# FNet mixing and a gated convolution FFN on one core: the last multiply-add a step later, the taps first, batch 1's folds moved

## The chip, the core and the metric

The kernel runs on one core of one Trainium2 chip. The metric is the device time of one execution in microseconds, as a median of several runs. TensorE (PE) multiplies matrices into PSUM, VectorE (DVE), ScalarE (ACT) and GpSimd (POOL) work on tiles, and SyncE (SP) issues transfers. Each engine runs its own instructions in the order in which they were written and waits on semaphores for the others.

## The reference

```python
X = np.fft.fft(np.fft.fft(x, axis=1), axis=2).real        # x: (8, 3136, 256)
h = np.maximum(X @ w_in, 0)                               # w_in: (256, 1024)
conv = cw[0]*h[s-1] + cw[1]*h[s] + cw[2]*h[s+1]           # along the sequence, zeros outside
gate = 1 / (1 + np.exp(-conv))
out = (h * gate) @ w_out                                  # w_out: (1024, 256)
```

## The kernel before

All arithmetic is float32. The weights arrive as float64 words and are narrowed to float32 on the core (`narrow`), in parts of four or so VectorE instructions and one of ScalarE.

*Per batch.* A batch of x (3136 x 256) comes in two halves, tiles `xh`: a plain load from SyncE, four gathers of mirrored rows issued by GpSimd (line 132), and for the second half three small loads of row 0 (`zero`, line 126). `fold_ops` gives sixteen VectorE steps, eight for each half, that add and subtract mirrored rows and features (lines 157 to 227); before `turned` ScalarE scales a copy (`scaled`). The result, tile `w`, goes through `units`: matrix products with cosine and sine tables (`tabs`, even and odd), put together on VectorE into `pt` and `qt`, the half-spectrum of the batch. Half of the spectrum is enough, since the other half mirrors it.

*The loop.* The DFT along the features and w_in are multiplied once into `G`. The loop has 256 steps (8 batches x 4 chunks of the sequence x 8 blocks of 128 rows of d_ff). Step s passes through:

| stage | engine | line |
|---|---|---|
| `seed` and `products`: `pa`, `pb` in PSUM | ACT, PE | 760, 93 |
| `copies`, `combine`: `nb`, then the row `h` (with relu) | ACT, DVE | 796, 805 |
| `first_tap`: `g` = tap 0 times h | ACT | 811 |
| `middle`: h added into g by an accumulating DMA (the taps are divided by the middle one) | POOL queue | 815 |
| `last_tap`: the last multiply-add of the convolution | DVE | 820 |
| `sigmoid`, `gate` (GpSimd takes half the row, VectorE the other) | ACT, POOL, DVE | 835, 843, 844 |
| `mm2`: the last product with w_out into `po` | PE | 93 |

The order in which these are written in iteration t is fixed by hand:

```python
    for t in range(n + LAG):                 # LAG = 4
        sigmoid(steps[t - 3]); run("first")
        products(steps[t + 1]); copies(steps[t + 1]); run("act")
        combine(steps[t]); seed(steps[t + 2]); first_tap(steps[t])
        run("dve"); last_tap(steps[t - 2]); gate(steps[t - 3])
        row_of(steps[t + 1]); middle(steps[t]); run("pool"); run("load")
        mm2(steps[t - LAG]); run("pe")
```

`run(...)` puts in what was entered for this iteration with `at(cycle, where, fn)`: the next batch's loads, folds and units, the remaining narrowing of the weights, and the "feature" work (one feature column for all batches). For batch 1 the sixteen folds stand in the free cycles from 4 to 23.

*The prologue.* Batch 0's work comes ahead of the loop. In the order written: `w_cv.load` (the conv taps, on ACT), the first part of w_in (SP), x's two halves, `load_turn` (angles, four loads of single words on ACT, line 287), a ScalarE instruction that negates the angles (line 699), three memsets on GpSimd, the odd tables of one kind (ACT, `load_odd`, lines 274 to 279), the even tables (SP, lines 260 to 265), the odd tables of the other kind (SP), then w_in's rest. After that `w_cv.narrow`, `w_in[0].narrow` and `taps` (a transposing product, the ScalarE copy of line 736 and small VectorE instructions, lines 738 to 744), and then the folds of batch 0. `scaled` writes four tiles from the pool `rp` for batch 0 (`parted`). After the folds `mend_row` and `mirror_tables` (lines 295 and 301) finish the tables on ScalarE, and TensorE runs the units.

Of the kernel before, what the change touches and what calls it, by code (L numbers as in the profile page):

```python
# [37 lines left out]
def kernel(  # L38
# [38 lines left out]
    hp = ctx.enter_context(tc.tile_pool(name="hp", bufs=5))  # L77
    gp = ctx.enter_context(tc.tile_pool(name="gp", bufs=6))
# [63 lines left out]
    def fold_ops(b):  # L142
# [4 lines left out]
        def half(h):  # L147
# [95 lines left out]
    rp = ctx.enter_context(tc.tile_pool(name="rp", bufs=4))  # L243
# [439 lines left out]
    def raw_in(i):  # L683
        def f(sh):
# [6 lines left out]
            for i in range(4)]  # L691
    w_cv.load(nc.scalar)
# [6 lines left out]
    act(turn[0:NP, 2], turn[0:NP, 1], AF.Copy, scale=-1.0)  # L699
# [12 lines left out]
    cw = const.tile([P, 3, NF], F32, name="cw")  # L712
# [20 lines left out]
    def taps():  # L733
        p = spare()
        mm(p[:, 0:3 * NF], cw24[:, 0], ident, True, True)
        nc.scalar.copy(out=cw.rearrange("p k m -> p (k m)"), in_=p[:, 0:3 * NF])
        small = const.tile([P, NF], F32, name="small")
        vt(small, cw[:, 1], cw[:, 1], op=ALU.mult)
        nc.vector.tensor_scalar(out=small, in0=small, scalar1=TINY * TINY, scalar2=2.0 * TINY, op0=ALU.is_lt,
                                op1=ALU.mult)  # L740
        vt(cw[:, 1], cw[:, 1], small, op=ALU.add)
        nc.vector.reciprocal(out=small, in_=cw[:, 1])
        for k in (0, 2):
            vt(cw[:, k], cw[:, k], small, op=ALU.mult)
# [17 lines left out]
    def triple(s):  # L762

        return third(steps.index(s))

    def third(i):

        return False

# [6 lines left out]
    def products(s):  # L776
        b, c, f = s
        ch, n, fs = cut(s)
        pb[s] = psb.tile([P, 512], F32, name="pb", tag="pb")
        mm(pb[s][:, 0:n], G[0:P - 1, 1, fs], PQ[b][1][0:P - 1, ch.k0:ch.k1], True, True)  # L780
        mm(pa[s][:, 0:n], G[:, 0, fs], PQ[b][0][:, ch.k0:ch.k1], False, not triple(s))
        if triple(s):
            mm(pa[s][:, 0:n], G[0:P - 1, 1, fs], PQ[b][1][0:P - 1, ch.k0:ch.k1], False, True)

    def copies(s):

        ch, n, fs = cut(s)
        p = pb.pop(s)
        nb[s] = nbp.tile([P, 2, HN], F32, name="nb", tag="nb")
        if triple(s):  # L790
            act(nb[s][:, 1, ch.cols], p[:, ch.cols], AF.Copy, scale=-2.0)
            row_of(s)
            act(hs[s][:, ch.front], pa[s][:, ch.fcols], AF.Relu)
        else:
            for i, cols in enumerate((ch.fcols, ch.cols)):
                act(nb[s][:, i, cols], p[:, cols], AF.Copy, scale=-1.0 if i else 1.0)  # L796

    def combine(s):

        ch, n, fs = cut(s)  # L800
        a, c = pa.pop(s), nb.pop(s)
        h = hs[s]
        for i, (to, cols) in enumerate(((h[:, ch.front], ch.fcols), (h[:, ch.back][:, ::-1], ch.cols))):
            if i or not triple(s):
                nc.vector._custom_dve(TENSOR_ADD_SAT, out=to, in0=a[:, cols], in1=c[:, i, cols],  # L805
                                      s0=BIG, s1=0.0)
# [15 lines left out]
    def shares(s):  # L822


        ch = chunks[s[1]]
        w = ch.w - 2
        n = ch.rest[0] if ch.last else w
        m = n - n // (4 if third(steps.index(s) + 2) else 2)
        return slice(0, m), slice(m, n), slice(n, w)
# [44 lines left out]
    w_cv.narrow(0, 1)  # L874
    w_in[0].narrow(0, 2)
    taps()
# [119 lines left out]
    for b in range(1, B):  # L996
        ops, singles, pres = fold_ops(b)
        c0, n = ends[b - 1], ends[b] - ends[b - 1]
        if b == 1:

            cs = [c for c in range(4, ends[1] + 1) if c not in taken]
            assert len(cs) == len(ops) and cs[len(ops) // 2] > NF + 4
# [16 lines left out]
    LAG = 4  # L1019
# [7 lines left out]
    for t in range(n + LAG):  # L1027
# [3 lines left out]
        if 0 <= t - 3 < n:  # L1031
            sigmoid(steps[t - 3])
# [94 lines left out]
```

## Time and profile before

| | us |
|---|---|
| three runs | 1188.72, 1190.26, 1190.9 (median 1190.26) |
| the profiled execution | 1192.42, of which its span is 1190.7 |
| busy in the span: PE, DVE, ACT, POOL | 1138.7, 957.9, 945.0, 600.7 |
| granted clock of TensorE, mean | 0.998 |
| read from and written to HBM | 38.40 MB, 25.74 MB |

The page of the profile gives the busy time of each engine and slices of the span; other views give the busy time in chosen stretches, an engine's instructions in order of time with the idle time before each and what ended it, and the waits summed by who waited for whom. An engine that is not the last one waited for may idle without cost.

### The profile page before, as it was taken

Reading aid. Unit: us, or ns where it says so; the run is one execution under the profiler, and the core shown is the slowest. Engines: PE = TensorE matmul, PEld = TensorE weight load, DVE = VectorE, ACT = ScalarE, POOL = GpSimd, SP = SyncE. Lnnn points to the kernel's source line nnn. Section 1 sums busy time; section 2 is a strip of 40 time slices with the busy share of each in tenths; the row PEclk is TensorE's granted clock in tenths of the full one; section 3 lists DMA queues with packets and bytes.
Section 4 is the critical chain, followed back from the end, with each engine's and each line's share of the span. In section 5 each row is a group of like instructions: output and inputs, shape, how many; then the busy total and the mean of one; then the engine's idle time right before and its main releaser. Section 6 shows DMA issues by size and latency. Waiting matters only on the chain.

```text
span 1190.7 us, 16046 instructions
## 1 busy us (share of the span) xinstructions
PE 1138.7 (96%) x4818; PEld 888.1 (75%) x4818; DVE 957.9 (80%) x1448; ACT 945.0 (79%) x1939; POOL 600.7 (50%) x734
## 2 busy tenths in 40 slices
PE   0989899999999999999999999999999999999998
PEld 0656678778777787777778777777777777777776
DVE  3689878988788798988787788998787687787774
ACT  0388777887888788888787888888887888898885
POOL 4335765666364546565646464454444444444443
PEclk9999999999999999999999999999999999999999
DMA  7386696767587667767766576765566556666664
GB/s 200 107 153 134 144 161 159 154 139 156 118 193 148 144 122 169 159 149 154 160 137 138 120 173 141 168 142 122 120 124 123 120 121 137 132 131 129 125 122 103
DMA packets 107586, 168.15 MB, mean 141 GB/s; under 512 B 32657, under 2 KB 62627, under 8 KB 107501
## 3 DMA queue, kind: packets, MB, share of 16 engines
q0 software_dynamic: 41984, 115.83, 51.4%
q1 hardware_dynamic: 64345, 50.89, 15.0%
q8 instruction: 38, 0.62, 0.2%
q10 hardware_dynamic: 1172, 0.43, 0.2%
q14 instruction: 47, 0.39, 0.1%
HBM read 38.40 MB, written 25.74 MB: 54 GB/s over the span
## 4 chain that ended last, share of the span: by engine, by line
PE 79%; ACT 7%; DVE 6%; issue 4%; POOL 2%; DMA 2%; ACTq 0%; POOLq 0%; DVEq 0%; SPq 0%
PE po L93 50%; PE pb L93 12%; PE pa L93 11%; PE pd L93 6%; ACT g L835 2%; DVE g L820 2%; ACT nb L796 2%; POOL xh L132 1%; DMA g<-h 1%; ACT os L868 1%; ACT g L811 1%; DMA out_dram<-os 1%; ACT pa L760 1%; DVE xh L168 0%; DVE g L844 0%
## 5 line engine op out<-in xcount | busy, mean ns | idle before, releaser
L93 PE MATMUL po<-wout,g 128*128 128x256 f32 x3072 | 707.2, 380 | 11.1 <-DVE g L844 10.5
L93 PEld LDWEIGHTS po<-wout,g 128*128 128x128 f32 x3072 | 580.1, 190 | 158.2 <-DVE g L844 28.1
L815 POOL DMA_DIRECT2D g<-h x256 | 228.1, 891 | 470.2 <-ACT g L811 244.7
L835 ACT ACTIVATE g<-g,cw 128x385 f32<-128x385 f32 (+2 forms) x512 | 292.0, 623 | 86.6 <-DVE g L820 85.7
L820 DVE SCALAR_TENSOR_TENSOR g<-h,cw,g 128x770 f32<-128x770 f32 (+1 forms) x256 | 299.1, 1168 | 41.7 <-DMA g<-h 41.6
L843 POOL TENSOR_TENSOR g<-g,h 128x385 f32<-128x385 f32 (+1 forms) x256 | 292.7, 1143 | 54.9 <-ACT g L835 53.8
L796 ACT ACTIVATE nb<-pb 128x386 f32<-128x386 f32 (+3 forms) x512 | 226.6, 497 | 93.9 <-PE pb L93 93.3
L805 DVE CUSTOM_DVE_ANT_0 h<-pa,nb 128x386 f32<-128x386 f32 (+3 forms) x512 | 264.2, 556 | 15.7 <-POOL h L774 11.4
L811 ACT ACTIVATE g<-h,cw 128x770 f32<-128x770 f32 (+1 forms) x256 | 244.0, 953 | 0.0
L93 PE MATMUL pb<-qt,G 127*128 127x387 f32 (+2 forms) x512 | 213.9, 499 | 2.3 <-ACT nb L796 1.3
L93 PE MATMUL pa<-pt,G 128*128 128x387 f32 (+2 forms) x512 | 211.9, 494 | 1.7 <-ACT pa L760 1.7
L844 DVE TENSOR_TENSOR g<-g,h 128x385 f32<-128x385 f32 (+1 forms) x256 | 172.9, 675 | 17.9 <-ACT g L835 17.9
L760 ACT ACTIVATE pa<-eb,ge 128x387 f32<-128x387 f32 (+2 forms) x256 | 155.0, 606 | 3.8 <-DVE h L805 3.5
L93 PEld LDWEIGHTS pa<-pt,G 128*128 128x128 f32 x512 | 96.8, 189 | 75.8 <-issue 16.5
L132 POOL DMA_INDIRECT xh<-in_x_dram,idx x64 | 94.8, 1481 | 18.7 <-issue 13.4
L93 PE MATMUL pd<-tab,w 98*128 98x197 f32 (+2 forms) x448 | 98.2, 317 | 1.0 <-POOL w L181 1.0
L93 PEld LDWEIGHTS pb<-qt,G 127*128 127x128 f32 x512 | 90.8, 190 | 8.6 <-ACT nb L796 2.3
L93 PEld LDWEIGHTS pd<-tab,w 98*128 98x128 f32 (+1 forms) x448 | 82.0, 191 | 10.4 <-POOL w L181 1.4
L868 ACT COPY os<-po 128x256 f32<-128x256 f32 x196 | 57.7, 393 | 7.9 <-PE po L93 4.5
L157 DVE TENSOR_TENSOR xh<-xh 98x1020 f32<-98x1020 f32 (+1 forms) x32 | 47.6, 1492 | 0.0
L168 DVE TENSOR_TENSOR xh<-xh 98x1024 f32<-98x1024 f32 (+1 forms) x32 | 44.8, 1400 | 0.1
L227 DVE SCALAR_TENSOR_TENSOR w<-w,turn,rt 98x256 f32<-98x256 f32 x28 | 12.6, 491 | 25.3 <-ACT rt L221 21.3
(140 smaller groups left out, 425.1 us busy)
## 6 DMA issues: line engine op xcount, KB each, us to landing
g<-h POOLq DMA_DIRECT2D x192, 385.0 KB, 4.0
g<-h POOLq DMA_DIRECT2D x64, 416.0 KB, 4.2
out_dram<-os SPq DMA_DIRECT2D x192, 128.0 KB
xh<-in_x_dram SPq DMA_DIRECT2D x16, 784.0 KB
eb<-ed SPq DMA_DIRECT2D x16, 193.5 KB
raw<-in_moe_w_in_dram SPq DMA_DIRECT2D x4, 512.0 KB
raw<-in_moe_w_out_dram SPq DMA_DIRECT2D x1, 2048.0 KB
eb<-ed SPq DMA_DIRECT2D x8, 209.0 KB
```

What stands on the lines that cost most here:

```text
L93: nc.tensor.matmul(o, l, r, start=start, stop=stop, skip_group_check=True)
L132: nc.gpsimd.indirect_dma_start(out=xh[b, h][0:NP, 7 - m].rearrange("p q d -> p (q d)"), out_offset=None, in_=bass.AP(tensor=x.tensor, offs ...
L760: act(pa[s][:, 0:n], eb[b, c], AF.Copy, scale=ge[:, f:f + 1])
L796: act(nb[s][:, i, cols], p[:, cols], AF.Copy, scale=-1.0 if i else 1.0)
L805: nc.vector._custom_dve(TENSOR_ADD_SAT, out=to, in0=a[:, cols], in1=c[:, i, cols], s0=BIG, s1=0.0)
L811: act(gs[s], hs[s][:, 0:n], AF.Copy, scale=cw[:, 0, s[2]:s[2] + 1])
L815: nc.gpsimd.dma_start(out=gs[s], in_=hs[s][:, 1:1 + n], accum_op=ALU.add)
L820: stt(out=g, in0=h[:, k:k + n], scalar=cw[:, k, f:f + 1], in1=g, op0=ALU.mult, op1=ALU.add)
L835: act(gs[s][:, c], gs[s][:, c], AF.Sigmoid, scale=cw[:, 1, s[2]:s[2] + 1])
L843: gt(g[:, p], g[:, p], h[:, p], op=ALU.mult)
L844: vt(g[:, v], g[:, v], h[:, v], op=ALU.mult)
L868: nc.scalar.copy(out=osb[:, j % 2], in_=pt[:, j % 2])
```

## The change

Four things are altered; the arithmetic stays the same.

1. `LAG` is 5: `last_tap` is written for step t - 3, `sigmoid` and `gate` for t - 4, `mm2` for t - 5. The pools for `h` and `g` have one buffer more each.
2. In the prologue `load_turn` is issued ahead of the zero-row loads, and narrowing and `taps` come ahead of the negated angles, the tables and the folds. One memset covers both kinds of odd table. Even tables are issued ahead of both odd ones, and SyncE's odd tables are written ahead of ScalarE's.
3. `parted` lies in tiles of the pool `h`; `rp` has two buffers and not four.
4. In the loop w_out is narrowed in iterations 4, 6, 8 and 10 (before 3, 5, 7, 9), batch 1's second half is loaded one iteration later, and batch 1's folds have a list of their own, from 9 to 22. A branch that was never taken (`triple`) is gone.

```diff
-    hp = ctx.enter_context(tc.tile_pool(name="hp", bufs=5))
-    gp = ctx.enter_context(tc.tile_pool(name="gp", bufs=6))
+    hp = ctx.enter_context(tc.tile_pool(name="hp", bufs=6))
+    gp = ctx.enter_context(tc.tile_pool(name="gp", bufs=7))
...
-                            parted[h, i // 2] = rp.tile([P, 2, 2, P], F32, name="rt", tag="rt")
+                            parted[h, i // 2] = hp.tile([P, HW], F32, name="h", tag="h")[:, 0:4 * P].rearrange(
+                                "p (a s d) -> p a s d", a=2, s=2)
...
-    rp = ctx.enter_context(tc.tile_pool(name="rp", bufs=4))
+    rp = ctx.enter_context(tc.tile_pool(name="rp", bufs=2))
...
     w_cv.load(nc.scalar)
     w_in[0].load(nc.sync)
-    for h in range(2):
-        for f in load_ops(0, h, nc.sync, nc.scalar, h == 1):
-            f()
-
+    for f in load_ops(0, 0, nc.sync):
+        f()
     load_turn(nc.scalar)
+    for f in load_ops(0, 1, nc.sync, nc.scalar, True):
+        f()
+
+    w_cv.narrow(0, 1)
+    w_in[0].narrow(0, 2)
+    taps()
     act(turn[0:NP, 2], turn[0:NP, 1], AF.Copy, scale=-1.0)
     nc.gpsimd.memset(tabs[0][0:1, 0, 0, 0:1], 0.0)
-    nc.gpsimd.memset(tabs[1][0:1, 1, 0, 0:1], 0.0)
+    nc.gpsimd.memset(tabs[1][0:1, 0:2, 0, 0:1], 0.0)
     nc.gpsimd.memset(tabs[1][96:KR, 0:2, 0], 0.0)
-    load_odd(nc.scalar, 1)
     load_even()
     load_odd(nc.sync, 0)
+    load_odd(nc.scalar, 1)
...
-    w_cv.narrow(0, 1)
-    w_in[0].narrow(0, 2)
-    taps()
...
-    for cycle, w_, c in ((0, w_in[2], 0), (2, w_in[3], 0), (3, w_out, 0), (5, w_out, 2), (7, w_out, 4), (9, w_out, 6)):
+    for cycle, w_, c in ((0, w_in[2], 0), (2, w_in[3], 0), (4, w_out, 0), (6, w_out, 2), (8, w_out, 4), (10, w_out, 6)):
...
-        at(NF + 2 + max(j - 2, 0), "load", fn)
+        at(NF + 3 + max(j - 2, 0), "load", fn)
...
-            cs = [c for c in range(4, ends[1] + 1) if c not in taken]
+            cs = [9, 11, 11, 12, 12, 13, 14, 14, 16, 17, 17, 18, 19, 20, 21, 22]
...
-    LAG = 4
+    LAG = 5
...
-        if 0 <= t - 3 < n:
-            sigmoid(steps[t - 3])
+        if 0 <= t - 4 < n:
+            sigmoid(steps[t - 4])
...
-        if 0 <= t - 2 < n:
-            last_tap(steps[t - 2])
         if 0 <= t - 3 < n:
-            gate(steps[t - 3])
+            last_tap(steps[t - 3])
+        if 0 <= t - 4 < n:
+            gate(steps[t - 4])
```

More of the change, by code (lines that the diff above doesn't have):

```diff
@@ L731, in column @@
         nc.scalar.copy(out=ge[:, i * NF // 4:(i + 1) * NF // 4], in_=p[:, 0:NF // 4])
[L733 to L744, printed above, removed]
     rows = out.rearrange("b s d -> (b s) d")
@@ L760, in seed @@
         act(pa[s][:, 0:n], eb[b, c], AF.Copy, scale=ge[:, f:f + 1])
[L762 to L768, printed above, removed]
     def row_of(s):
@@ L789, in copies @@
         nb[s] = nbp.tile([P, 2, HN], F32, name="nb", tag="nb")
[L790 to L796, printed above, removed]
+        for i, cols in enumerate((ch.fcols, ch.cols)):
+            act(nb[s][:, i, cols], p[:, cols], AF.Copy, scale=-1.0 if i else 1.0)
     def combine(s):
@@ L803, in combine @@
         for i, (to, cols) in enumerate(((h[:, ch.front], ch.fcols), (h[:, ch.back][:, ::-1], ch.cols))):
-            if i or not triple(s):
-                nc.vector._custom_dve(TENSOR_ADD_SAT, out=to, in0=a[:, cols], in1=c[:, i, cols],
-                                      s0=BIG, s1=0.0)
+            nc.vector._custom_dve(TENSOR_ADD_SAT, out=to, in0=a[:, cols], in1=c[:, i, cols],
+                                  s0=BIG, s1=0.0)
     def first_tap(s):
@@ L827, in shares @@
         n = ch.rest[0] if ch.last else w
-        m = n - n // (4 if third(steps.index(s) + 2) else 2)
+        m = n - n // 2
         return slice(0, m), slice(m, n), slice(n, w)
@@ L999 @@
         if b == 1:
-            cs = [c for c in range(4, ends[1] + 1) if c not in taken]
-            assert len(cs) == len(ops) and cs[len(ops) // 2] > NF + 4
+            cs = [9, 11, 11, 12, 12, 13, 14, 14, 16, 17, 17, 18, 19, 20, 21, 22]
+            assert len(cs) == len(ops) and cs[-1] <= ends[1] and not taken & set(cs)
         else:
```

18 lines of the change are left out of this document (14 added, 4 removed).

## The prediction

> **What bounds the kernel now.** I read the stages first, then the order of time of each engine in the first 60 us, then the waits of the loop. Columns of the stages: stretch, its length, busy us and instructions of PE, PEld, DVE, ACT and POOL, granted clock, DMA share, GB/s.
>
> ```profile
> 0.00:24.50 24.50, 0.59 (x2) 0.50 (x2) 6.57 (x20) 1.67 (x3) 11.67 (x27) 1.00 0.87 214
> 24.50:42.10 17.60, 11.14 (x28) 5.84 (x28) 17.27 (x24) 5.39 (x14) 5.24 (x8) 1.00 0.35 110
> 60.00:81.00 21.00, 17.34 (x72) 11.32 (x72) 16.44 (x30) 17.53 (x37) 5.84 (x11) 1.00 0.97 164
> 81.00:164.00 83.00, 75.67 (x308) 55.89 (x309) 72.89 (x114) 67.92 (x149) 54.20 (x60) 1.00 0.71 146
> 200.00:600.00 400.00, 395.95 (x1681) 309.96 (x1680) 338.17 (x520) 329.30 (x671) 229.76 (x264) 1.00 0.70 151
> 600.00:1186.00 586.00, 585.62 (x2470) 461.38 (x2468) 468.22 (x671) 489.98 (x995) 272.95 (x338) 1.00 0.64 132
> ```
>
> From 600 us to 1186 TensorE is never out of work (585.6 of 586.0), and from 200 to 600 it lacks 4.0 us. No edit of order can shorten that part; the end moves only with the time at which TensorE begins the loop and with its idle time before 200 us. The prologue splits in two: up to 24.5 us VectorE does 6.6 us of work, then it folds batch 0 of x without a pause. Why it starts so late is seen in ScalarE's order of time, and then in VectorE's (start, length, line, tiles; in brackets the idle time before and what ended it):
>
> ```profile
> 1.46 2.21 ACTq L126 DMA_DIRECT2D xh<-in_x_dram  x3
> 5.26 5.64 ACTq L287 DMA_DIRECT2D turn<-dft_seq_dram  x4
> 18.30 1.28 ACT L699 ACT_TABLE_LOAD   x1 [18.30 <-DMA turn<-dft_seq_dram]
> 22.67 0.62 ACTq L279 DMA_DIRECT2D tab<-dft_seq_dram  x1
> 23.33 0.18 ACT L736 COPY cw<-po 128x24 f32<-128x24 f32 x1 [3.54 <-DMA tab<-dft_seq_dram]
> ```
> ```profile
> 8.66 0.69 DVE L636 SCALAR_TENSOR_TENSOR win<-raw,win 128x512 f32<-128x512 f32 x1
> 23.54 0.17 DVE L738 TENSOR_TENSOR small<-cw 128x8 f32<-128x8 f32 x1 [14.19 <-ACT cw L736]
> 24.55 2.34 DVE L157 TENSOR_TENSOR xh<-xh 98x1020 f32<-98x1020 f32 x2
> 33.25 2.35 DVE L157 TENSOR_TENSOR xh<-xh 99x1020 f32<-99x1020 f32 x2
> 41.36 0.68 DVE L195 TENSOR_TENSOR w<-xh 99x508 f32<-99x508 f32 x1
> ```
>
> VectorE is free at 9.35, but its next work is the conv taps, which need ScalarE's copy L736. That copy stands on ScalarE behind the negated angle (L699), which waits for the turn loads until 18.30, and behind four issues of the odd tables. So the folds, in order behind the taps, wait 14.2 us for a copy of 128x24. They end at 42.04, and what follows hangs on them:
>
> ```profile
> 40.92 1.19 ACT L301 ACTIVATE tab<-tab 99x196 f32<-99x196 f32 x4
> 42.16 0.60 PE L93 MATMUL po<-tab,w 98*128 98x196 f32 x2 [1.91 <-ACT tab L301]
> 59.95 0.92 PE L93 MATMUL pb<-qt,G 127*128 127x386 f32 x2 [0.46 <-DVE win L618]
> ```
>
> TensorE resumes at 42.16 and starts the loop at 59.95.
>
> **Part 1, taps ahead of the angles and the folds.** No instruction is removed. In the built order of the changed kernel ScalarE issues the taps' load, four turn loads and three zero-row loads; the second zero load waits for the semaphore of x's first half, the third for that of the first turn load; then come the activation table, the copy L736, and only then the angle and the odd tables. So the copy still stands behind two landings. Their price:
>
> ```profile
> L132 POOL DMA_INDIRECT xh<-in_x_dram,idx x8: 966/982/1222, 2.2 to 11.8; - x8
> DMA to landing us min/median/max: 5.4/7.0/8.8
> turn<-dft_seq_dram ACTq DMA_DIRECT2D x4, 0.4 KB
> 1.27 6.38 SPq L119 DMA_DIRECT2D xh<-in_x_dram  x2
> 12.85 4.45 SPq L260 DMA_DIRECT2D tab<-dft_seq_dram  x2
> 25.46 0.68 SPq L276 DMA_DIRECT2D tab<-dft_seq_dram  x1
> ```
>
> The trace shows no landing of the first turn load by itself. The four were all issued by 10.90 (5.26 + 5.64) and the last landed at 18.30, which is 7.4 us. An issue takes 0.74 (2.21 for three), so the first turn load, issued second on ScalarE after 0.75 + 0.67, is out at about 2.2 and lands at about 9.6. Then: last zero load 0.7, table load 1.28, copy 0.18, which is 11.8, and 1.2 from the copy to the first fold (23.33 to 24.55): folds start at **13.0**, not 24.55, a gain of **11.5 us**. Bounds: earliest is VectorE's own 9.35 plus 1.2, about 10.6 (gain 13.9); latest is ScalarE held until 18.30 as now, which makes the folds start at 18.30 + 0.7 + 1.28 + 0.18 + 1.2 = 21.7 (gain 2.9). I take 13.0, since the 7.4 us belongs to the same kind of load.
>
> [...]
>
> Is x there? The eight gathers of x's mirrored rows are issued by GpSimd from 2.2 to 11.8, four for each half, and take 5.4 to 8.8 to land. The first two serve the first fold instruction and are in by 12.5 at the latest (issued 2.2 and 3.7); the last of the second half is in by 11.8 + 8.8 = 20.6 (the plain loads, the second issued by 7.65, show no landing; with the gathers' 8.8 it is in by 16.5), and the second half's folds would start at 33.25 - 11.5 = 21.75. Both lie inside, the second with 1.1 to spare; should it be short, only that shortage is lost. The tables are next. In the kernel before, SyncE's second even table waits until 16.7 (4.45 for the two issues), since its semaphore was in use by a load of x; now it waits for a turn load. ScalarE's odd tables go out behind GpSimd's memsets of that tile (about 13.4) and no longer at 18.4. TensorE needs the odd tables for good when ScalarE has mirrored them: 42.16 - 11.5 = 30.7. Even if they land as late as now they are in by then (SyncE issues the last of them by 26.14, and ScalarE used them at 40.92 without a wait). I cost the order of the tables at nothing; with that cover gone it would be a microsecond or two. The fold results' holder changes from its own pool to the h pool; h's first rows in the loop come long after TensorE has read them, so that costs nothing as well.
>
> **Part 2, the last multiply-add a step later.** Sigmoid, gate and the last product all follow one step later, so between gate and product nothing changes; only the transfer that adds the middle tap gets one more step. Price and return come from these rows (chain of waits near the end, for a dense step; then waits: TensorE's for the gate from 60 to 164 us, two of TensorE's from 164 to the end, two of VectorE's from 60 to 164; total, times, longest):
>
> ```profile
> 1153.36 0.70 PE pb L93 x2
> 1154.06 0.71 PE pa L93 x2
> 1154.77 2.59 PE po L93 x12
> ```
> ```profile
> PE po L93 <- DVE g L844: 6.8, 8, 1.4
> PE po L93 <- DVE g L844: 3.7, 6, 1.0
> PE pd L93 <- POOL w L181: 1.0, 1, 1.0
> DVE w L227 <- ACT pa L760: 4.1, 1, 4.1
> DVE g L820 <- DMA g<-h: 3.7, 2, 2.8
> ```
>
> A dense step takes TensorE 4.0 us, 2.6 of it the last product. With five steps of lag, one last product more lies undone when the loop's start-up is over: **+2.6**. Nothing is given back at the end, where TensorE has no gap now. In return VectorE has done one multiply-add and one gate less at any step, and it no longer waits 3.7 us (60 to 164 us) for two transfers. Of these two waits the shorter, 0.9, falls where VectorE is the limit and counts whole; the longer, 2.8, reached TensorE as about 1.2 (one of the eight waits for the gate, at most 1.4 each): **-2.1**. After 164 us six waits for the gate cost 3.7; I credit the one behind a late transfer, **-1.2**.
>
> **Part 3, batch 1's folds in steps 9 to 22.** Sixteen operations stood in steps 4 to 23, about one a step; steps 11, 12, 14 and 17 now hold two, and steps 4, 6 and 8 none (the narrowing of w_out goes there instead). VectorE's groups between 81 and 164 us:
>
> ```profile
> L820 DVE SCALAR_TENSOR_TENSOR g<-h,cw,g 128x770 f32<-128x770 f32 x18 | 19.6, 1088 | 3.7 <-DMA g<-h 3.7
> L844 DVE TENSOR_TENSOR g<-g,h 128x385 f32<-128x385 f32 x19 | 10.4, 549 | 0.0
> L805 DVE CUSTOM_DVE_ANT_0 h<-pa,nb 128x386 f32<-128x386 f32 (+1 forms) x37 | 18.8, 547 | 0.8 <-POOL g L843 0.8
> L168 DVE TENSOR_TENSOR xh<-xh 98x1024 f32<-98x1024 f32 (+1 forms) x4 | 5.6, 1398 | 0.0
> L157 DVE TENSOR_TENSOR xh<-xh 98x1020 f32<-98x1020 f32 (+1 forms) x4 | 5.2, 1304 | 0.0
> L195 DVE TENSOR_TENSOR w<-xh 98x508 f32<-98x508 f32 (+1 forms) x3 | 3.1, 1035 | 0.0
> ```
>
> A step costs VectorE 1.09 + 0.55 + 2 x 0.55 = 2.7, with one fold 4.0 to 4.1, with two 5.3 or so. TensorE needs 4.0. So VectorE stays the limit up to about step 17 and TensorE from there; up to step 22 the folds' total is the same in both orders. What remains of VectorE's side is the one multiply-add and gate less, 1.09 + 0.55: **-1.6**. Fold ends at step 22 and no longer in 23, where TensorE's batch-1 unit waited 1.0 for the memset behind it: **-1.0**. The wait of 4.1 (the turning on VectorE waits for ScalarE, which by the order written has output copies and feature tables ahead of it) moves from step 12 to 13 along with the output copies; I take it as unchanged.
>
> The sum: -11.5 + 2.6 - 2.1 - 1.2 - 1.6 - 1.0 = **-14.8 us**. The profiled execution took 1192.42 (span 1190.7 and 1.7 around it), 2.2 above the median of the three runs, 1190.26; the sum taken off that execution is 1177.6, and off the median **1175.5 us**. Bounds of the loop: +1.0 if VectorE limits every step up to 22 (2.6 - 1.6), -8 if the 4.1 us wait and the rest of TensorE's waits for the gate go as well.
>
> **Rivals.** *The turn loads hold ScalarE until 18.30.* For it: they are four loads of single words, and 18.30 is what the trace shows for their end. Against: the copy waits for the first of the four alone. Time: 1190.26 - 2.9 - 3.3 = 1184.1.
>
> *The loop gives nothing.* Two folds in a step come while VectorE is the limit, so it limits all steps up to 22, and the waits removed reappear there: -11.5 + 1.0, 1179.8. For it: 72.9 of 83 us busy already. Against: single-fold steps 18 to 22 cost no more than TensorE's 4.0.
>
> *Slower: folds and GpSimd block each other.* Folds read two tiles in SBUF, and GpSimd's half of the gate reads SBUF in the same steps. In the loop L195 takes 1.04 in the mean, and in the prologue, with GpSimd idle, 0.68. If each of the 17 fold instructions that now stand in steps 9 to 17 were longer by 1.0 more than today, +17 on the limiting engine, the result is 1190.26 - 11.5 + 1.0 + 17 = 1196.8. It decides from a lengthening of 0.6 each (10.5 over 17); today's is 0.36 for L195, and L157 shows 0.13 (1.30 against 2.34 for two in the prologue). [...]
>
> *The change doesn't reach the start.* If the tables or x's second half, not the folds, were what the start waits for, only the loop's +1.0 to -3.3 would show, about 1189.
>
> **How the numbers follow.** Forecast 0.66, turn loads 0.10, loop gives nothing 0.12, folds blocked 0.08, start not reached 0.04. The three first are faster by over 0.2% (2.4 us, about what a measurement can tell): 0.88; same 0.04; slower 0.08. The range runs from 1169.5 (13.9 in the prologue and half of the loop's way to -8) to 1184.5, which takes in the second and third case and leaves out the last two.
>
> **What would show it.** Right: the copy of the taps near 12 us, folds starting at 12 to 14 and ending near 30.5, the loop's first product near 48.5, no wait of VectorE for the middle tap's transfer in the loop's first 100 us, and TensorE's first last-product at about the same distance from the loop's start as now, or up to 3 us more. Wrong: the copy after 18 us; folds that start early but pause before the second half; TensorE waiting for tables at 26 to 31 us; more waits for the gate in steps 9 to 17 than the 6.8 us now.

## The result and the profile after

| | us |
|---|---|
| before, nine runs | median 1190.26 (1188.63 to 1191.96) |
| after, nine runs | median 1186.99 (1184.92 to 1188.7) |
| ratio after to before | 0.9971, 95% interval 0.996 to 0.9981 |
| forecast | 1175.5, range 1169.5 to 1184.5 |
| profiled execution after | 1188.70, span 1186.9 |

The change made the kernel 3.3 us faster, where 14.8 were forecast. The profiled execution is the longest of the nine and the one with the lowest granted clock; the shortest, at 1184.92, is still 9.4 us above the forecast. The stages of the changed kernel, with the columns of the prediction's first fence:

```profile
0.00:24.50 24.50, 8.25 (x15) 3.90 (x16) 18.44 (x35) 3.27 (x7) 14.26 (x31) 1.00 0.86 214
24.50:42.10 17.60, 15.92 (x93) 13.92 (x92) 9.61 (x20) 8.18 (x21) 3.43 (x6) 0.90 0.39 117
60.00:81.00 21.00, 17.15 (x65) 11.70 (x65) 16.70 (x30) 17.64 (x35) 9.11 (x20) 0.92 0.75 107
81.00:164.00 83.00, 75.18 (x310) 55.36 (x309) 76.23 (x115) 65.04 (x144) 45.95 (x51) 1.00 0.72 141
200.00:600.00 400.00, 397.27 (x1692) 312.04 (x1691) 339.74 (x523) 333.14 (x676) 220.77 (x266) 1.00 0.69 149
600.00:1183.00 583.00, 577.93 (x2428) 454.07 (x2426) 460.43 (x653) 480.63 (x977) 276.39 (x332) 1.00 0.62 131
```

VectorE now works 18.4 us of the first 24.5 (6.6 before): the folds have moved forward. But between 81 and 164 us TensorE is no busier than before (75.2 of 83, against 75.7), and after 600 us it now lacks 5.1 us (583.00 - 577.93), of which 0.95 lie behind its last product, which ends at 1182.05; before it lacked 0.4, of which 0.23 lay behind its last product. The granted clock is 0.90 and 0.92 in two stages that ran at 1.00.

The prologue in order of time, ScalarE, VectorE, TensorE (L698 is the taps' copy, L736 before; L700 the first small VectorE instruction of the taps, L738 before):

```profile
9.77 1.28 ACT L698 ACT_TABLE_LOAD   x1 [9.77 <-issue]
11.06 0.18 ACT L698 COPY cw<-po 128x24 f32<-128x24 f32 x1
...
11.28 0.17 DVE L700 TENSOR_TENSOR small<-cw 128x8 f32<-128x8 f32 x1 [1.95 <-ACT cw L698]
12.28 2.35 DVE L157 TENSOR_TENSOR xh<-xh 98x1020 f32<-98x1020 f32 x2
20.99 2.35 DVE L157 TENSOR_TENSOR xh<-xh 99x1020 f32<-99x1020 f32 x2
29.11 0.68 DVE L195 TENSOR_TENSOR w<-xh 99x508 f32<-99x508 f32 x1
...
45.30 3.60 PE L93 MATMUL po<-win,dm 128*128 128x256 f32 x8
49.37 0.92 PE L93 MATMUL pb<-qt,G 127*128 127x386 f32 x2 [0.46 <-DVE win L619]
```

The copy stands at 11.06 and no longer at 23.33, the folds start at 12.28 and no longer at 24.55, and they don't pause before the second half. The loop's first product is at 49.37, 10.6 us earlier than 59.95. Nearly all that is missing is lost behind that point. The stretches from the loop's first product to the end of the first group of twelve last products (`po` from `wout`), from there to the end of the 17th group, and from there to TensorE's last product, show it, before and then after (columns as above):

```profile
59.95:84.23 24.28, 20.24 (x85) 13.92 (x86) 19.72 (x35) 20.63 (x42) 6.80 (x13) 1.00 0.93 159
84.23:158.39 74.16, 67.20 (x271) 48.88 (x271) 65.46 (x102) 60.46 (x134) 49.27 (x55) 1.00 0.68 146
158.39:1185.77 1027.38, 1022.15 (x4333) 803.69 (x4331) 840.76 (x1251) 849.66 (x1728) 522.41 (x625) 1.00 0.67 140
...
49.37:77.49 28.12, 23.10 (x89) 15.42 (x90) 20.17 (x36) 22.85 (x46) 7.89 (x15) 0.94 0.84 137
77.49:152.96 75.47, 67.65 (x272) 48.84 (x271) 71.35 (x105) 61.14 (x136) 43.17 (x52) 1.00 0.67 146
152.96:1182.05 1029.09, 1022.24 (x4328) 803.78 (x4327) 839.80 (x1245) 847.82 (x1722) 519.99 (x623) 1.00 0.66 139
```

From the loop's first product on, TensorE takes 6.9 us longer: 1132.7 and no longer 1125.8. Its idle time there (length less busy time) went from 16.2 to 19.7 us. Its busy time, for the same products, went from 1109.6 to 1113.0, since two stretches of this execution ran at a granted clock of 0.50 (the last section shows them).

The table gives the same at a finer grain, with times that are worked out from the trace of one execution of each kernel: the loop's first product (`pb`), the start of the first group of last products, then the lengths from the end of the 1st group to that of the 17th, from there to the 33rd, the 61st and the 256th.

| | loop's first product | first group | 1st to 17th | 17th to 33rd | 33rd to 61st | 61st to 256th |
|---|---|---|---|---|---|---|
| before | 59.95 | 81.37 | 74.2 | 77.9 | 124.3 | 824.7 |
| after | 49.37 | 73.42 | 75.5 | 76.6 | 123.2 | 828.9 |

The forecast saw the loop's first steps get shorter (by 1.6 + 2.1 to about the 17th group) and the rest shorter by 2.2; both got longer.

### The profile page after: what moved, and what is told of

It reads as the page before. It is cut to its first block, busy times and chain, and to the rows that moved or that the text cites. A ratio compares the mean times of both kernels' runs of the same rounds, so it can differ in the third digit from the quotient of the medians.

```text
span 1186.9 us, 16040 instructions
## 1 busy us (share of the span) xinstructions
PE 1144.0 (96%) x4818; PEld 890.8 (75%) x4818; DVE 963.0 (81%) x1448; ACT 945.9 (80%) x1939; POOL 594.2 (50%) x734
## 4 chain that ended last, share of the span: by engine, by line
PE 70%; ACT 7%; DVE 6%; issue 3%; DMA 2%; POOL 2%; SPq 0%; ACTq 0%; DVEq 0%; POOLq 0%
PE po L93 44%; PE pb L93 11%; PE pa L93 10%; PE pd L93 5%; DVE g L811 2%; ACT g L826 2%; ACT nb L788 2%; ACT os L859 1%; DMA out_dram<-os 1%; POOL g L834 1%; DVE h L796 1%; DMA eb<-ed 1%; POOL xh L132 1%; ACT pa L767 1%; DMA xh<-in_x_dram 1%
## 5 line engine op out<-in xcount | busy, mean ns | idle before, releaser
L826 ACT ACTIVATE g<-g,cw 128x385 f32<-128x385 f32 (+2 forms) x512 | 291.5, 621 | 77.7 <-DVE g L811 75.2
L834 POOL TENSOR_TENSOR g<-g,h 128x385 f32<-128x385 f32 (+1 forms) x256 | 287.6, 1124 | 56.9 <-ACT g L826 55.4
L811 DVE SCALAR_TENSOR_TENSOR g<-h,cw,g 128x770 f32<-128x770 f32 (+1 forms) x256 | 288.1, 1125 | 0.0
L835 DVE TENSOR_TENSOR g<-g,h 128x385 f32<-128x385 f32 (+1 forms) x256 | 188.0, 734 | 25.3 <-ACT g L826 25.0
L132 POOL DMA_INDIRECT xh<-in_x_dram,idx x64 | 91.8, 1434 | 18.6 <-issue 11.5
L168 DVE TENSOR_TENSOR xh<-xh 98x1024 f32<-98x1024 f32 (+1 forms) x32 | 44.2, 1382 | 0.1
L194 DVE TENSOR_TENSOR w<-xh 98x508 f32<-98x508 f32 (+1 forms) x32 | 33.5, 1047 | 0.2
```

Of the source, the lines that this page charges most:

```text
L132: nc.gpsimd.indirect_dma_start(out=xh[b, h][0:NP, 7 - m].rearrange("p q d -> p (q d)"), out_offset=None, in_=bass.AP(tensor=x.tensor, offs ...
L811: stt(out=g, in0=h[:, k:k + n], scalar=cw[:, k, f:f + 1], in1=g, op0=ALU.mult, op1=ALU.add)
L826: act(gs[s][:, c], gs[s][:, c], AF.Sigmoid, scale=cw[:, 1, s[2]:s[2] + 1])
L834: gt(g[:, p], g[:, p], h[:, p], op=ALU.mult)
L835: vt(g[:, v], g[:, v], h[:, v], op=ALU.mult)
```

## The experiments

Each kernel was timed in five rounds beside the kernel before; "against before" is the ratio to those runs, with its 95% interval. Kernels e1 to e4 share their runs of before (median 1190.92), as do e5 to e8 (1191.03), e9 to e12 (1190.4) and e13, e14 (1190.81).

**e1, the prologue alone** (point 2 of the change, made in the kernel before; all diffs of this section are shortened):

```diff
+    w_cv.narrow(0, 1); w_in[0].narrow(0, 2); taps()
     act(turn[0:NP, 2], turn[0:NP, 1], AF.Copy, scale=-1.0)
...
-    w_cv.narrow(0, 1); w_in[0].narrow(0, 2); taps()    # were behind all loads
```

> The kernel before with the prologue's part alone: turn loads, narrowing and taps first, even tables first; lag 4 and batch 1's folds as before. Theory A (the prologue's 12 us arrive at the loop and the other two parts of the change give 6 to 8 of them back): 10 to 12 us faster than before, more than the whole change's 3.3. Theory B (what is won ahead of the loop is lost in it whatever else is done, since half-clock windows of TensorE or something bound to absolute time eats it): 3 to 5 us faster, about the whole change's time, with a granted clock of 0.997 or less where before has 0.998.

Measured: 1177.01 us, 0.9883 (0.9866 to 0.99), 13.9 us less than before, so theory A holds for the prologue. The loop's first product stands at 46.39. This part alone is worth more than the whole change.

**e2, the lag alone** (points 1 and 3):

```diff
-    LAG = 4
+    LAG = 5
-            last_tap(steps[t - 2]) ... gate(steps[t - 3])
+            last_tap(steps[t - 3]) ... gate(steps[t - 4])
```

> The kernel before with lag 5 alone (the pools for h and g one buffer larger, batch 0's turned parts in h tiles). Theory A: 3 to 6 us slower than before: one product more undone at the start (2.6), and SyncE's stores of the output now stand behind the next batch's load, which costs some us in the steady part. Theory B: within 1 us of before, or faster.

Measured: 1198.17 us, 1.006 (1.0046 to 1.0074), 7.2 us more, more than either theory had. By its trace the stretch from the 1st to the 17th group is shorter (70.4 us, before 74.2), but the first group starts at 82.99 (before 81.37) and the 61st to the 256th take 829.4 (before 824.7): the lag gives in the middle and takes at both ends.

**e3, point 4 alone** (folds and w_out's narrowing):

```diff
-    ... (3, w_out, 0), (5, w_out, 2), (7, w_out, 4), (9, w_out, 6)
+    ... (4, w_out, 0), (6, w_out, 2), (8, w_out, 4), (10, w_out, 6)
-            cs = [c for c in range(4, ends[1] + 1) if c not in taken]
+            cs = [9, 11, 11, 12, 12, 13, 14, 14, 16, 17, 17, 18, 19, 20, 21, 22]
```

> The kernel before with batch 1's folds in steps 9 to 22, w_out narrowed in 4, 6, 8, 10 and batch 1's second half loaded a step later; lag 4 and the prologue as before. Theory A: 0 to 2 us faster (1.0 for the unit that waited for the last fold; the stretch stays bound by VectorE). A rival: 2 to 4 us slower, because two folds in a step hold VectorE while TensorE waits for the gate.

Measured: 1197.28 us, 1.0057 (1.0041 to 1.0072), 6.4 us more, outside both forecasts. In order of time, TensorE and VectorE of e3 (L495 prepares the feature tables, L636 ends the narrowing of one part of w_out):

```profile
82.95 4.54 PE L93 MATMUL po<-wout,g 128*128 128x256 f32 x12 [3.90 <-DVE wout L636]
96.28 4.42 PE L93 MATMUL po<-wout,g 128*128 128x256 f32 x12 [3.59 <-DVE wout L636]
...
82.21 0.69 DVE L636 SCALAR_TENSOR_TENSOR wout<-raw,wout 128x512 f32<-128x512 f32 x1
91.82 0.17 DVE L495 TENSOR_SCALAR ft<-ft 128x2 int32<-128x2 int32 x1 [5.10 <-POOL ft L493]
```

With the lag still 4, the last product of step 0 is written in iteration 4, the very one that now narrows the part of w_out that it needs; it waits 3.9 us, and the third group again 3.6. So e3 does not measure the folds: point 4 leans on point 1. VectorE also waits 5.1 us for GpSimd at the feature tables in iteration 5, which no narrowing covers any more.

**e4, the change without the lag** (points 2 and 4, the diffs of e1 and e3 together):

> The changed kernel without the longer lag (prologue and folds changed, lag 4). Theory A: 10 to 13 us faster than before, some 8 faster than the changed kernel, so that the lag alone is what costs. Theory B: 3 to 5 us faster than before, as the changed kernel.

Measured: 1186.12 us, 0.9958 (0.9943 to 0.9973), 9.1 us more than e1, with the same two waits for w_out (3.9 and 3.6 us). That is theory B's time: this loss is there without the lag. Hence e5.

**e5, e1 with late folds and early narrowing** (batch 1's load also stays where it was):

```diff
     ... (3, w_out, 0), (5, w_out, 2), (7, w_out, 4), (9, w_out, 6)      # as before
+            cs = [10, 11, 11, 12, 12, 13, 14, 14, 16, 17, 17, 18, 19, 20, 21, 22]
```

> The prologue part, with batch 1's folds moved to steps 10 to 22, but w_out's narrowing left in steps 3, 5, 7 and 9 and the loads where they were; lag 4. In the kernel with the folds moved and the narrowing a step later, the first gated matmuls waited 4.1 and 3.8 us in the steps where w_out's tables were narrowed in the same step that needs them. Theory C (the late narrowing, not the folds' place, cost the 9.1 us on top of the prologue): 1176 to 1180 us, no wait of 3 us or more at the first and third gated matmuls, and VectorE's 5 us wait for GpSimd's iota gone. Theory D (folds crowded into fewer steps cost by themselves): 1183 to 1187 us, with TensorE waiting for the gate in steps 10 to 22.

Measured: 1179.3 us, 0.9907 (0.9893 to 0.9922). Theory C holds: most of e4's 9.1 us was the narrowing (the load of batch 1's second half, which moved back with it, was not tried alone); the folds by themselves are within 2.3 us of e1, and the intervals overlap.

**e6, e1 with the lag** (the diffs of e1 and e2):

> The prologue part and the lag of five steps, folds and narrowing where they were. Lag alone cost 7.2 us and folds alone 6.4, on top of each other less. If the parts' costs add: 1177.0 + 7.2 = 1184.2 us, with output stores queued behind the next batch's loads on SyncE (waits of 2 to 3 us at batches' ends), and the first gated matmuls 2.6 us later. Rival: the prologue's order already took up what the lag costs, 1178 to 1181 us.

Measured: 1186.78 us, 0.9963 (0.9949 to 0.9977), as long as the whole change and more than either forecast. So at lag 5 there is a loss that folds and narrowing don't make. It is not made up as that of the change is: e6 is shorter from the 1st to the 17th group and longer after the 61st (the table below). After 164 us it is seen in the changed kernel around 650 us (ScalarE, VectorE, TensorE in order of time):

```profile
649.20 0.37 ACT L859 COPY os<-po 128x256 f32<-128x256 f32 x1 [3.19 <-DMA out_dram<-os]
649.47 1.12 ACT L826 ACTIVATE g<-g,cw 128x385 f32<-128x385 f32 x2
651.24 0.33 ACT L405 COPY as<-pd 128x197 f32<-128x197 f32 x1
651.60 0.36 DVE L411 TENSOR_TENSOR as<-as,pd 128x196 f32<-128x196 f32 x1 [7.04 <-ACT as L405]
652.38 0.44 PE L93 MATMUL pd<-tab,w 99*128 99x99 f32 x2 [2.52 <-DVE as L412]
```

The copy of an output tile waits for the store that empties its buffer. Behind it on ScalarE stand the sigmoid and the copy of a unit (L405); VectorE waits 7.0 us for that, and TensorE 2.5 us for VectorE. With lag 4 the output copies of a batch's last step stood one iteration earlier against the unit and the loads. SyncE issues the stores in order behind the next load of x (L119), which waits for a fold, and this was taken to be what holds them up. SyncE's waits of the changed kernel (total, times, longest):

```profile
SPq L119 <- DVE w L195: 179.3, 10, 26.4
```

Before, the same row has 105.7 us in 7 waits, and TensorE has no wait above 1.1 us after 164 us.

**e7, the changed kernel with later loads:**

```diff
-                    at(cs[len(ops) // 2 * (h + 1) - 1] + 1 + j, "load", fn)
+                    at(cs[len(ops) // 2 * (h + 1) - 1] + 2 + j, "load", fn)
```

> The changed kernel with the later batches' loads of x one step later, so that each stands behind the same output stores on SyncE as before the change. Theory E (stores behind loads cost the two TensorE waits of 1.6 and 2.7 us near 370 and 650 us and the half-clock window of 1.7 us that followed the second): 1181 to 1184 us, both waits gone, the time after 164 us some 4 to 6 us shorter. Rival (the waits only move to another store): 1186 to 1188 us, as the changed kernel.

Measured: 1187.18 us, 0.9974 (0.9962 to 0.9985): no gain. TensorE's wait near 370 us is gone, that near 650 us is not, and the one near 240 us grew from 1.0 to 1.9 us. SyncE's row falls to 80.1 us in 6, yet the wait near 650 us stays at 2.5. Theory E is right for the wait near 370 us only.

**e8, e6 with the same later loads:**

> The prologue part, the lag of five steps and the later batches' loads one step later; folds and narrowing where they were. Theory E: 1177 to 1181 us, 3 to 6 us below the same kernel without the later loads. If the lag pays for itself once its stores are clear of the loads: below 1177.0 us, the best so far. Rival: no difference to the kernel without the later loads.

Measured: 1181.94 us, 0.9922 (0.9908 to 0.9936), 4.8 us less than e6 and just outside theory E's range; e6's trace has a granted clock of 0.50 from 647.7 to 654.5 us, and the mean granted clock of the two profiled executions is 0.994 and 0.997. SyncE's wait above falls to 75.0 us in 6. But near 640 us ScalarE still waits 3.2 us for a store: an odd batch ends with seven output tiles, in four pairs, and there are three buffers of two tiles. Hence e9.

**e9, e8 with seven single output tiles:**

```diff
-    osp = ctx.enter_context(tc.tile_pool(name="osp", bufs=3))
+    osp = ctx.enter_context(tc.tile_pool(name="osp", bufs=7))
...
-                osb = osp.tile([P, 2, D], F32, name="os", tag="os")
...
+                    osb = osp.tile([P, D], F32, name="os", tag="os")      # one for each copy
```

> The prologue part, lag 5 and later loads as before, with seven single output tiles in place of three pairs, so that the seven copies at the end of an odd batch need not wait for an output store. In the kernel without this ScalarE waited 3.2 us for a store at 640 us with the unit's copy, VectorE (6.1 us) and TensorE (2.7 us) queued behind it. Theory F (with the lag, the fourth pair's wait is what is left after 164 us): 1178 to 1180 us, TensorE's gaps near 643 and 647 us (2.7 and 0.8) gone. Rival (the lag's first waits, ahead of 164 us, are all of what is left): 1181.5 to 1182.5 us, no change.

Measured: 1177.61 us, 0.9895 (0.9879 to 0.9912). ScalarE's and TensorE's order of time at the same place of e9:

```profile
636.16 2.01 ACT L873 COPY os<-po 128x256 f32<-128x256 f32 x7
637.99 1.20 ACT L840 ACTIVATE g<-g,cw 128x385 f32<-128x385 f32 x2
639.76 0.40 ACT L405 COPY as<-pd 128x197 f32<-128x197 f32 x1
...
638.99 2.75 PE L93 MATMUL po<-wout,g 128*128 128x256 f32 x12
641.58 0.36 PE L93 MATMUL pd<-tab,w 99*128 99x99 f32 x2
```

All seven copies run in a row, and TensorE goes on without a wait. Theory F holds, with a time slightly below its range: the wait near 650 us came from the number of output buffers, not from the loads. From the 61st to the 256th group e9 takes 823.2 us, e6 831.2, the changed kernel 828.9, the kernel before 824.7. So lag 5 with later loads and more output buffers is 1.5 us shorter than before after the 61st group. No run has these two mends at lag 4, so what they alone would give there is not shown; the wait near 650 us does not occur in the traces of before and e1.

**e10, e9 with the sigmoid's table loaded at the start, and e11, e1 with that alone:**

```diff
+    warm = const.tile([P, 1], F32, name="warm")
+    act(warm, low, AF.Sigmoid)
     w_cv.narrow(0, 1)
```

It goes back to this wait of the changed kernel (ScalarE, TensorE in order of time):

```profile
67.48 1.28 ACT L826 ACT_TABLE_LOAD   x1
68.77 1.12 ACT L826 ACTIVATE g<-g,cw 128x385 f32<-128x385 f32 x2
69.80 0.70 ACT L621 ACTIVATE wout<-wout,low 128x512 int32<-128x512 int32 x1
70.42 0.84 ACT L788 ACTIVATE nb<-pb 128x385 f32<-128x385 f32 x2
...
71.31 0.92 PE L93 MATMUL pb<-qt,G 127*128 127x386 f32 x2 [2.64 <-ACT nb L788]
73.42 4.07 PE L93 MATMUL po<-wout,g 128*128 128x256 f32 x12 [0.30 <-DVE g L835]
```

> As the kernel with seven output tiles, and a one-element sigmoid on ScalarE ahead of the taps, so that the sigmoid's table is loaded once, at the start, and not at 66.6 us ahead of the first product's copies. Theory G (the table load of 1.28 us makes the TensorE wait of 2.9 us at 66 us, and the half-clock window of 3.4 us behind it follows from that wait): 1174 to 1177 us, the wait down to 1.7 us and the window gone. Rival (the wait has its cause in the first multiply-adds and copies ahead of it): the load's 1.28 us alone or less, 1177 to 1179 us.

> The prologue part alone with the same one-element sigmoid at the start. At lag 4 the table load at 61.0 us stands beside the narrowing of VectorE (61.4 to 66.7 us), so theory G expects little: 1175.5 to 1177.5 us. If ScalarE is what the first gate waits for there: 1.3 us less, 1175.5 us or below. If Copy needs another table than the sigmoid, one more load of 1.28 us and 1177 to 1179 us.

Measured: e10 1176.74 us, 0.9879 (0.9862 to 0.9895); e11 1178.39, 0.9895 (0.9879 to 0.9912). The second table load is gone in both. In e10 TensorE's wait went from e9's 2.8 us to 2.3 only, so theory G is mostly wrong about the wait, though no half-clock window followed it (the granted clock is 1.00 from 66 to 72.77 us, and the eight products at 73.36 took 1.99 us); e11 lies in the range of its third forecast, but not for its reason, since there is one load and not two; the 0.9 us between e9 and e10 and the 1.4 between e1 and e11 are within the intervals. In the rows above the load takes 1.28 us, and the sigmoid starts 1.29 us after the load's start.

**e12, the changed kernel with all three mends** (later loads, seven output tiles, early table):

> The changed kernel with the three mends together: later loads a step later, seven output tiles, the sigmoid's table loaded at the start. If stores and table load are what kept the change from its forecast: 1177 to 1180 us, with the gaps at 647 us and the wait of 2.8 us at 65 us gone. If the late folds and the narrowing beside them cost as much again: 1182 to 1185 us.

Measured: 1180.21 us, 0.991 (0.9894 to 0.9927), between its two forecasts. So the mends return about 7 us of the missing 11, and e10, which differs from e12 in the place of folds and narrowing (and of one load of batch 1), is 3.5 us shorter.

**e13 and e14, e10 with late folds or with late narrowing:**

```diff
# e13: narrowing in 3, 5, 7, 9
+            cs = [10, 11, 11, 12, 12, 13, 14, 14, 16, 17, 17, 18, 19, 20, 21, 22]
# e14: narrowing in 4, 6, 8, 10
+            cs = [5, 7, 9, 11, 12, 13, 14, 14, 16, 17, 18, 19, 20, 21, 22, 23]
```

> The fullest kernel so far (prologue part, lag 5, later loads, seven output tiles, early table load: 1176.74 us) with batch 1's folds in steps 10 to 22 and w_out's narrowing left in steps 3, 5, 7 and 9. From the end of the first group of gated products to that of the 33rd the traces have 152.0 us before, 148.6 in the fullest kernel, 152.4 with the late folds and the late narrowing. Theory H (the late narrowing takes the gain away): 147 to 149 us for the stretch, 1175 to 1177 us in all. Theory K (the late folds, two to a step in steps 11, 12, 14 and 17, take it away beside the lag): 151 to 153 us for the stretch, 1179 to 1181 us in all.

> The fullest kernel with w_out's narrowing in steps 4, 6, 8 and 10 and batch 1's folds in the steps free beside it (5, 7, 9, 11 to 14, two in 14, 16 to 23), so nearly where they were. Theory H: 151 to 153 us for the stretch from the first to the 33rd group, 1179 to 1181 us in all. Theory K: 148 to 149.5 us for the stretch, 1176 to 1178 us in all.

Measured: e13 1179.35 us, 0.9907 (0.9892 to 0.9922); e14 1178.84, 0.9899 (0.9884 to 0.9914). TensorE's waits for VectorE's half of the gate from 81 to 164 us, in e10, e13, e14 and e12, a fence each:

```profile
PE po L93 <- DVE g L851: 2.9, 4, 1.0
```
```profile
PE po L93 <- DVE g L851: 5.8, 8, 1.4
```
```profile
PE po L93 <- DVE g L851: 4.7, 6, 1.8
```
```profile
PE po L93 <- DVE g L837: 7.8, 9, 1.8
```

The same table as in the section on the result, with VectorE's busy time from the end of the 1st to that of the 17th group beside it (before 65.5, after 71.4):

| | loop's first product | first group | 1st to 17th | 17th to 33rd | 33rd to 61st | 61st to 256th | VectorE busy, 1st to 17th |
|---|---|---|---|---|---|---|---|
| e1 | 46.39 | 67.83 | 74.1 | 77.9 | 124.1 | 825.0 | 65.3 |
| e6 | 47.85 | 71.86 | 70.4 | 77.8 | 124.3 | 831.2 | 61.2 |
| e9 | 46.09 | 69.63 | 70.4 | 77.8 | 123.5 | 823.2 | 62.2 |
| e10 | 49.57 | 73.36 | 70.8 | 77.8 | 123.6 | 823.3 | 62.5 |
| e12 | 47.65 | 70.42 | 75.8 | 76.6 | 123.9 | 823.3 | 70.5 |
| e13 | 46.19 | 69.20 | 75.2 | 76.6 | 123.9 | 823.2 | 71.0 |
| e14 | 47.74 | 70.51 | 73.6 | 78.0 | 123.6 | 823.3 | 64.3 |

From the first group to the 33rd, e10 takes 148.6 us, e13 151.8, e14 151.6, e12 152.4. Neither theory is right alone: either move by itself takes back about 3 of the 3.4 us that the lag gains there, and the second adds less than 1. In the whole time the difference of 2 to 3 us has the same sign, but the intervals overlap; the lengths and the waits carry the verdict. The traces show how. TensorE's longest wait for a gate in the changed kernel (step 8) stands behind an iteration with two folds, in VectorE's order of time (L194, L195 and L168 are folds, L811 the last multiply-add, L835 the gate) and TensorE's:

```profile
106.66 1.22 DVE L194 TENSOR_TENSOR w<-xh 98x508 f32<-98x508 f32 x1
107.80 1.35 DVE L195 TENSOR_TENSOR w<-xh 98x508 f32<-98x508 f32 x1
109.07 1.21 DVE L168 TENSOR_TENSOR xh<-xh 98x1024 f32<-98x1024 f32 x1
110.21 1.01 DVE L811 SCALAR_TENSOR_TENSOR g<-h,cw,g 128x770 f32<-128x770 f32 x1
111.14 0.55 DVE L835 TENSOR_TENSOR g<-g,h 128x385 f32<-128x385 f32 x1
...
111.74 1.56 PE L93 MATMUL po<-wout,g 128*128 128x256 f32 x6 [1.72 <-DVE g L835]
```

In the same way the gates of steps 2, 4 and 6 stand behind a part of w_out's narrowing. And between the ends of the 1st and the 17th group VectorE has more to do: the traces count 19 fold instructions there before (19.3 us), 21 in e9 and e10 (19.7), and 24 in the changed kernel (24.9), e12 and e13 (24.3 each); the narrowing takes 8.7 us there before, 6.5 in e10 and 10.6 in the changed kernel. Of batch 1's 26 fold instructions one stands ahead of this stretch and six behind it in the kernel before, none and two in the changed kernel. In e14 VectorE is little busier than in e10 (64.3 against 62.5 us), so there the amount does not explain the late gates; the place of the narrowing is what is left, since the folds stand nearly where they were.

## Why the prediction was wrong

*The prologue: right, a little small.* Forecast were folds at 13.0, their end near 30.5 and the loop's first product near 48.5, for 11.5 us; measured 12.28, 29.8 (29.11 + 0.68) and 49.37. The turn loads, the tables and x's second half held up nothing, so the rivals of the start fall. The folds moved by 12.3 us, the loop's first product by 10.6 only: the traced execution has two half-clock stretches ahead of it (the eight products at 45.30 took 3.60 us; those at 57.52 before, 1.97), that of before has one (0.51 from 43.25 to 46.66 us). In e1 the folds start at 12.59, and with no such stretch (granted clock 1.00) the first product comes 13.6 us earlier.

*The lag's fill of 2.6: the distance came, but it was not the cost.* The first group stands 24.05 us behind the loop's first product, before 21.42. But the prediction held that nothing is given back at the end. With a lag of five steps one more pair of products `pb` and `pa` (0.70 + 0.71 in a dense step) stands ahead of the first group, and so one pair less behind the 17th. That part of the 2.6 is work done earlier. TensorE's idle time up to the end of the first group rose by 1.0 us only (4.0 to 5.0). The half-clock stretch at 72.5, in no term, cost some 1.4 more by estimate (the first group took 4.07 us; 2.86 in e1).

*VectorE's relief of 1.6 + 2.1 in the loop's first steps: right for the lag, wrong for the change.* VectorE no longer waits for the middle tap's transfer in 60 to 164 us, as forecast. Lag 5 with the old order of folds and narrowing (e6, e9) shortens the stretch from the 1st to the 17th group by 3.8 us, near the 3.7 of those two terms; TensorE's idle time there falls from 7.0 to 3.8. In the changed kernel the stretch is 1.3 us longer. The step that failed is the sentence that "up to step 22 the folds' total is the same in both orders", by which part 3 was costed at nothing on VectorE. The total up to step 22 is the same, but by the prediction's own reading VectorE is the limit only to about step 17, and a gate waits for what stands ahead of it in its own iteration. Between the 1st and the 17th group VectorE was busy for 71.4 us and not 65.5, and TensorE's waits for the gate from 60 to 164 us went from 6.8 to 8.0 us, from eight to eleven, the sign that the prediction had named for this:

```profile
PE po L93 <- DVE g L835: 8.0, 11, 1.7
```

*After 164 us, -1.2 and -1.0: both waits fell, but others came that had no term.* TensorE's waits for the gate there fell from 3.7 to 2.0 us, and the 1.0 for the memset is gone. In their place it waits 1.5 us near 372 and 2.5 at 652, the latter with a half-clock stretch behind it (0.50 from 652.75 to 656.15). Idle time from the 17th group on rose from 5.2 to 6.9 us, and the stretch is 1.7 us longer (1027.4 before, 1029.1 after) although it holds one pair of products less. The prediction followed each queue that the prologue's edits pass, but not that of the lag: with `mm2` an iteration later, the output copies and stores also move an iteration, behind a load on SyncE and in front of a unit's copy on ScalarE, and three output buffers no longer suffice. It wrote "between gate and product nothing changes" and did not ask what follows the product; of the part after 600 us it asked only whether it could get shorter. With later loads and seven output tiles (e9), this part is 1025.0: 1.4 of the 2.4 us gained is the pair of products that moved forward, and TensorE's idle time falls by 0.9, against the 2.2 that were forecast (e9 keeps the old folds, so the 1.0 is not in it).

*Half-clock stretches: in no term.* Up to TensorE's last product the changed kernel's traced execution has four (0.50 each), that of before one (43.3 us); that of e1 has none (1.00 in every stretch up to 1170 us). The two in the loop are the 3.4 us by which TensorE's busy time grew. This execution has the lowest mean clock of its nine (0.994; the others 0.995 to 0.999), so by their clocks this share is smaller in the others.

*The sum.* In the profiled executions the loop was to become 3.3 us shorter and became 6.9 longer. Of these 10.2 us, 4.6 are idle time from the 1st to the 17th group (+0.9 for -3.7), 3.8 idle time behind it (+1.6 for -2.2) and 3.4 half clock, less the 1.6 by which the fill was priced too high. TensorE's idle time from the loop's first product on, in us:

| | to the end of the 1st group | to that of the 17th | to the last product | sum |
|---|---|---|---|---|
| before | 4.0 | 7.0 | 5.2 | 16.2 |
| after | 5.0 | 7.8 | 6.9 | 19.7 |
| e6 | 4.9 | 3.8 | 9.8 | 18.4 |
| e9 | 4.9 | 3.8 | 4.3 | 12.9 |
| e12 | 4.0 | 8.0 | 3.7 | 15.7 |

e9, with the lag mended and the old folds, has 3.3 us less than before, just the loop's forecast sum, but that is partly luck: the fill was priced too high and the return after 164 us as well. That e10 comes to 1175.9 us (0.9879 of 1190.26) against the forecast 1175.5 is partly luck too, since e10 holds mends that the forecast did not know of, and e1 without any lag is as short. The low end of the range was also added up wrongly: 13.9 in the prologue and half of the way from -3.3 to -8 in the loop give 1170.7, not 1169.5.

The rival of folds and GpSimd blocking each other, the only slower one, did not come: batch 1's 26 fold instructions take 24.4 us in all before and 26.3 after, 1.9 more and not 17. The 1.04 us for L195 before is the mean of 0.67, 1.75 and 0.68; the 1.75, at 129.92, stands beside GpSimd's half of a gate (130.21, 0.91 us). In the prologue GpSimd was not idle beside the 0.68 at 41.36: its copy L202 ran from 41.43 for 0.66 us. *The loop gives nothing* had the sign of what happened, but not its place or size (+1.0, measured +6.9).

The shortest are e10 and e1 (0.9879 and 0.9883 of before, not to be told apart); both beat the changed kernel by about 10 us. e1 does it with one part of the change. So a gain of the lag in the whole time is not shown; only its stretches are shorter.

## What to carry to other kernels

A step that is moved takes everything behind it along: when the last product moves an iteration, follow its output copy and store into the queues where they now stand behind a load or ahead of another's work, and count the buffers for the fullest iteration. Work of equal total is not of equal cost: what counts is how much of it falls into the stretch in which its engine is the limit, and what stands ahead of the one instruction that the bounding engine waits for. So count moved work over that stretch alone, and bound its price from the waits for that instruction. When a pipeline gets a step longer, price the idle time of the bounding engine and not the later start of its last stage, for some of its work only moves forward. And cut a bundle into its parts: here one part gave 13.9 us, and the others took more than 10 of it back.

## What was not expected of the hardware

In some places TensorE's granted clock falls to 0.50 for a stretch (window) of 3.4 us. Windows of the changed kernel up to TensorE's last product (the granted clock is the third number from the end; the last two rows are the stretches ahead of the third and fourth):

```profile
31.55:34.96 3.41, 3.41 (x12) 3.41 (x12) 0.00 (x0) 0.00 (x0) 0.00 (x0) 0.50 0.56 214
45.20:48.60 3.40, 3.40 (x10) 2.61 (x9) 0.83 (x2) 0.53 (x2) 2.79 (x5) 0.50 1.06 377
72.50:75.90 3.40, 3.10 (x8) 2.04 (x7) 3.40 (x6) 3.07 (x7) 1.80 (x3) 0.50 0.53 98
652.75:656.15 3.40, 3.40 (x8) 1.95 (x8) 3.40 (x7) 2.03 (x6) 1.78 (x3) 0.50 0.47 89
...
69.13:72.54 3.41, 1.23 (x4) 0.68 (x4) 1.97 (x3) 3.41 (x7) 0.91 (x2) 0.99 0.48 89
649.37:652.78 3.41, 0.89 (x6) 0.52 (x5) 1.14 (x4) 3.41 (x8) 0.90 (x2) 1.00 0.36 112
```

Their starts are 13.65, 27.3 and 580.25 us apart, and 13.65 / 4, 27.3 / 8 and 580.25 / 170 are all 3.41: in this trace they lie whole lengths of a window apart. What TensorE did in the stretch ahead of each differs: 1.23 and 0.89 us of work in 3.41 were followed by half clock, as were 1.74 in 3.42 (28.12 to 31.54), and so was the stretch ahead of 45.2 (41.77 to 45.19), in which TensorE was busy throughout; 1.57 in 3.42 in e10 (69.35 to 72.77) were not. What decides is not shown. Each window costs, as an estimate, up to 1.7 us, half of 3.4; the eight products at 45.30 took 1.63 us longer than those before (3.60 against 1.97). The nine runs of the changed kernel go from a span of 1183.1 us at a mean clock of 0.999 to 1186.9 at 0.994. Of TensorE's waits, those of 2.64 us (to 71.31) and 2.52 (to 652.38) have a window behind them, e10's of 2.31 (to 71.19) has none. So, as an estimate, a wait of 2 to 3 us on TensorE costs its length and, at times, 1.7 us more. In the traces of e10 and the changed kernel the prologue has two such windows (in e10 the granted clock is 0.90 from 24.5 to 42 us and 0.94 from 42.4 to 45.8; in the changed kernel the first two rows above), in that of e13 none (1.00 up to 1170 us).
